# Modulation weights as eight row blocks on two DMA queues, summed block by block, at the start of a transformer-block kernel

## The chip, the cores and the metric

The kernel runs on one NeuronCore of one Trainium2 chip. The metric is the device time of one execution in microseconds (us); lower is better. A profile is one traced execution, and its span (first to last instruction) is about 1.9 us shorter than the device time of the same execution. Engine names: PE is TensorE, PEld its weight loads, DVE is VectorE, ACT is ScalarE, SP is SyncE, POOL is GpSimd. A "q" after an engine (SPq, ACTq) means its queue issuing DMA. PE and the DMA engines are the two actors of this story.

All runs below are of the fast state. They carry a second variation that matters here: the granted clock of PE over the span, between 0.992 and 1.000.

## The reference, cut to what matters

```python
mod = (silu(c) @ w_mod).reshape(1, 6, 1, -1)     # c: 1 x 1024, w_mod: 1024 x 6144, bf16
sa, ca, ga, sb, cb, gb = mod[:, 0..5]
h = layernorm(x) * (1 + ca) + sa                 # x: 2048 x 1024
x = x + ga * linear_attention(h @ wqkv) @ wo     # 32 heads
h = layernorm(x) * (1 + cb) + sb
x = x + gb * (silu(h @ w_gate) * (h @ w_up)) @ w_down
```

Nothing of the first projection can start before `sa` and `ca` are known for the rows of the contraction that it uses. Those two vectors need the first 2,048 columns of `w_mod`, 4 MB in bf16. That wait at the very start is what the change is about. (MB in the cost sums below are the loads' 1024 x 1024 bytes; KB are 1024 bytes.)

## The kernel before

The tokens are worked off in four chunks of 512; a chunk has four tiles of 128 tokens. The start-up (chunk 0) loads x tiles 0 to 2, c, and the modulation columns in *column blocks*: for each half b of the 1,024 columns and for q = 1 (ca) and q = 0 (sa), one load of all 1,024 rows by 512 columns. In such a load every contiguous piece is 1 KB.

```python
wme = [[big("wme", [DC, NB]) for _ in range(2)] for _ in range(2)]     # DC = 8, NB = 512

def load_mod(b, q, lo, hi):
    nc.sync.dma_start(out=wme[b][q][:, :, lo:hi], in_=wm_v[:, :, q * D + b * NB + lo:q * D + b * NB + hi])

load_mod(0, 1, 0, NB)      # ca, first half of the columns
load_mod(0, 0, 0, NB)      # sa, first half
load_k(0); load_k(1)       # 256 KB each: rows of wk
load_x(STC - 1, nc.sync)   # x tile 3
load_k(2); load_k(3)
load_mod(1, 1, 0, NB)      # second half of the columns, in between the rest of wk
load_mod(1, 0, 0, NB // 2)
# ... (cut)
```

PE turns silu(c) into column sums with matvecs (128x128 weights, one moving column). The column loop is outside, so a column needs all eight row groups j at once:

```python
def mod_block(b, q, lo, hi):
    for i in range(lo, hi):
        col = q * DC + 4 * b + i
        for j in range(DC):
            mm(mod_ps[:, col:col + 1], lhsT=wme[b][q][:, j, i * P:(i + 1) * P],
               rhs=scT[:, j:j + 1], start=(j == 0), stop=(j == DC - 1))
    # ... (cut: copy to ca1T with +1, or to saT)
```

With half of the columns modulated, PE starts the K projection on half of the contraction (four of eight row groups of wk, six of eight output groups), and fits the second half, and tile 3, in between:

```python
def keep_warm(acc, n):                       # warm-up matmuls: work whose result nobody reads
    for _ in range(n):
        mm(acc[:], lhsT=sel[:, 0, :], rhs=sel[:], start=True, stop=True)

# ... (cut: transposes of tiles 0 to 2, first half of the modulation)
k_mms(0, gs, accs, 0, 4)                     # 24 K matmuls
xn3 = ln1_norm(*ln1_stats(0, 3), dve=True)
pe_transpose_tile(hT, xn3, 3, DC // 2)
for cc in range(4):
    modulate(hT, cc, ca1T, saT, H, SCW)
mod_block(1, 1, 0, 4)                        # second half, between K matmuls
# ... (cut: 40 K matmuls more)
```

The start-up on VectorE, ScalarE and GpSimd is held to the program order, and in the timeline PE's matmuls stand in that order too. After the K projection of chunk 0 comes its V projection, and from there PE is never idle.

Of the kernel before, what the change touches and what calls it, by code (L numbers as in the profile page):

```python
# [8 lines left out]
ACT = mybir.ActivationFunctionType  # L9
ALU = mybir.AluOpType  # L10
BF16 = mybir.dt.bfloat16
F32 = mybir.dt.float32
# [9 lines left out]
def kernel(  # L22
# [13 lines left out]
    nc = tc.nc  # L36
    P = nc.NUM_PARTITIONS
    _, S, D = A_x.shape
# [4 lines left out]
    DC = D // P  # L43
    HG = DC
    FC = F // P
    SCW = 512
    NSC = S // SCW
    STC = SCW // P
    NB = 512
# [16 lines left out]
    wm_v = w_mod.rearrange("(j p) n -> p j n", p=P)  # L66
    c_v = c.rearrange("o (j p) -> (o j) p", p=P)

    const = ctx.enter_context(tc.tile_pool(name="const", bufs=1))
# [12 lines left out]
    @contextmanager  # L82
    def in_order(*engines):
        types = [e.engine for e in engines]
        traced = nc.cur_bb.bb.instructions
        mark = traced[-1]
        yield
        first = next(k for k in reversed(range(len(traced))) if traced[k] is mark) + 1
        for i in traced[first:]:
            if i.engine in types:  # L90
                prev = last_on.get(i.engine)
                if prev is not None:
                    tc.add_manual_dep(i, prev.name, mybir.DependencyInfo(
                        mybir.DependencyClass.NoSync, mybir.DependencyReason.DATA), reason="in_order")
                last_on[i.engine] = i

    def mm(out, lhsT, rhs, start, stop):
        return tc.keep_in_program_order(nc.tensor.matmul(out, lhsT=lhsT, rhs=rhs, start=start, stop=stop))  # L98

    def transpose(out, in_):  # L100
        return tc.keep_in_program_order(nc.tensor.transpose(out, in_, ident[:]))  # L101

    def big(name, shape):
        return k8.tile([P] + shape, BF16, name=name, tag="k8")

    def acc_a():
        return pa.tile([P, NB], F32, name="acc", tag="pa")

    def acc_b(name, shape=(NB,), dt=F32):
        return pb.tile([P] + list(shape), dt, name=name, tag="pb")  # L110
# [3 lines left out]
    c_sb = const.tile([DC, P], BF16, name="c_sb")  # L114
# [3 lines left out]
    def load_x(st, eng):  # L118
        x_sb = k2.tile([P, D], BF16, name="x_sb")
        eng.dma_start(out=x_sb[:], in_=x2[st * P:(st + 1) * P, :])  # L120
        x_tiles[st] = x_sb

    for st in range(STC - 1):
        load_x(st, nc.sync)
    nc.sync.dma_start(out=c_sb[:], in_=c_v)

    wk = [big("wk", [4, D]), big("wk", [4, D])]
    wme = [[big("wme", [DC, NB]) for _ in range(2)] for _ in range(2)]

    def load_mod(b, q, lo, hi):  # L130
        nc.sync.dma_start(out=wme[b][q][:, :, lo:hi], in_=wm_v[:, :, q * D + b * NB + lo:q * D + b * NB + hi])

    def load_k(cc):
        nc.sync.dma_start(out=wk[cc // 4][:, cc % 4, :], in_=wqkv_v[:, cc, D:2 * D])

    load_mod(0, 1, 0, NB)
    load_mod(0, 0, 0, NB)
    load_k(0)
    load_k(1)
    load_x(STC - 1, nc.sync)  # L140
    load_k(2)
    load_k(3)
    load_mod(1, 1, 0, NB)
    load_mod(1, 0, 0, NB // 2)
    load_k(4)
    load_k(5)
    load_mod(1, 0, NB // 2, NB)
    load_k(6)
    load_k(7)

    def load_w(view, lo, name):
        ts = []
# [11 lines left out]
    ident = const.tile([P, P], BF16, name="ident")  # L164
    make_identity(nc, ident[:])
    neg_half = const.tile([P, 1], F32, name="neg_half")
    nc.vector.memset(neg_half[:], -0.5)

    scT = const.tile([P, DC], BF16, name="scT")
    sc32 = const.tile([P, DC, 32], BF16, name="sc32")  # L170

    saT = const.tile([P, DC], F32, name="saT")
    ca1T = const.tile([P, DC], F32, name="ca1T")
    sbT = const.tile([P, DC], F32, name="sbT")
    cb1T = const.tile([P, DC], F32, name="cb1T")
    ga_t = ep.tile([P, NB], F32, name="e")
# [40 lines left out]
    def modulate(hT, cc, scaleT, biasT, lo=0, hi=SCW):  # L217
        nc.vector.tensor_scalar(out=hT[:, cc, lo:hi], in0=hT[:, cc, lo:hi], scalar1=scaleT[:, cc:cc + 1],  # L218
                                scalar2=biasT[:, cc:cc + 1], op0=ALU.mult, op1=ALU.add)

    def pe_transpose_tile(hT, xn, t, split):
        tp = acc_b("tp", (DC, P), BF16)
        for cc in range(DC):
            transpose(tp[:, cc, :], xn[:, cc * P:(cc + 1) * P])
        if split < DC:
            nc.scalar.copy(out=hT[:, split:DC, t * P:(t + 1) * P], in_=tp[:, split:DC, :])  # L226
        nc.vector.tensor_copy(out=hT[:, 0:split, t * P:(t + 1) * P], in_=tp[:, 0:split, :])

    hTs = {}

    def ln1_stats(sc, t):
        x_sb = x_tiles.pop(sc * STC + t)
        mv = small.tile([P, STC, 2], F32, name="mv")
        bn(x_sb, mv[:, 0, :])
        rstd = rstd_of(mv, 1)
        return sc, t, x_sb, mv, rstd

    def ln1_norm(sc, t, x_sb, mv, rstd, dve=False):
        xn = k2.tile([P, D], BF16, name="xn", bufs=4)
        if dve:  # L240
            normalise(xn[:], x_sb[:], mv[:, 0, 0:1], rstd[:, 0:1])
        else:
            normalise_act(xn[:], x_sb[:], mv, rstd)
        if sc > 0:
            nc.sync.dma_start_transpose(hTs[sc][:, :, t * P:(t + 1) * P], xn[:])
        return xn
# [3 lines left out]
        for t in range(STC):  # L250
            ln1_norm(*ln1_stats(sc, t))

    def mod_block(b, q, lo, hi):
        for i in range(lo, hi):
            col = q * DC + 4 * b + i
            for j in range(DC):
                mm(mod_ps[:, col:col + 1], lhsT=wme[b][q][:, j, i * P:(i + 1) * P],
                   rhs=scT[:, j:j + 1], start=(j == 0), stop=(j == DC - 1))
        cs = slice(4 * b + lo, 4 * b + hi)
        src = mod_ps[:, q * DC + 4 * b + lo:q * DC + 4 * b + hi]  # L260
        if q == 1:
            nc.vector.tensor_scalar_add(out=ca1T[:, cs], in0=src, scalar1=1.0)
        else:
            nc.vector.tensor_copy(out=saT[:, cs], in_=src)

    last_phi = [None]

# [11 lines left out]
    def k_mms(sc, gs, accs, cc_lo=0, cc_hi=DC):  # L279
        for cc in range(cc_lo, cc_hi):  # L280
            for (t, nb), acc in zip(gs, accs):
                mm(acc[:], lhsT=hTs[sc][:, cc, t * P:(t + 1) * P], rhs=wk[cc // 4][:, cc % 4, nb * NB:(nb + 1) * NB],
                   start=(cc == 0), stop=(cc == DC - 1))
# [129 lines left out]
    def keep_warm(acc, n):  # L413
        for _ in range(n):
            mm(acc[:], lhsT=sel[:, 0, :], rhs=sel[:], start=True, stop=True)

    gs = k_groups[0:6]
    accs = [acc_a() if i < 4 else acc_b("acc") for i in range(6)]
    spare = accs[5]
    keep_warm(spare, 11)  # L420
    hT = hTs[0] = big("hT", [DC, SCW])
    pks[0] = big("pk", [STC, D])
    H = 3 * P
    with in_order(nc.vector, nc.scalar, nc.gpsimd):
        mod_ps = acc_b("mod_ps")
        mm(mod_ps[:, 0:DC], lhsT=c_sb[:], rhs=ident[0:DC, 0:DC], start=True, stop=True)
        keep_warm(spare, 10)
        nc.scalar.activation(out=scT[:], in_=mod_ps[:, 0:DC], func=ACT.Silu)
        xns = [ln1_norm(*ln1_stats(0, t)) for t in range(3)]
        pe_transpose_tile(hT, xns[0], 0, DC)  # L430
        keep_warm(spare, 3)
        pe_transpose_tile(hT, xns[1], 1, DC)
        keep_warm(spare, 2)
        mod_block(0, 1, 0, 4)
        pe_transpose_tile(hT, xns[2], 2, DC // 2)
        keep_warm(spare, 4)
        for lo, hi in ((0, 1), (1, 4)):
            mod_block(0, 0, lo, hi)
            for cc in range(lo, hi):
                modulate(hT, cc, ca1T, saT, 0, H)  # L440
        k_mms(0, gs, accs, 0, 4)
        xn3 = ln1_norm(*ln1_stats(0, 3), dve=True)
        pe_transpose_tile(hT, xn3, 3, DC // 2)
        for cc in range(4):
            modulate(hT, cc, ca1T, saT, H, SCW)
        mod_block(1, 1, 0, 4)
        gs7, accs7 = k_groups[6:7], [acc_b("acc")]
        k_mms(0, gs7, accs7, 0, 2)
        for cc in (4, 5):
            mod_block(1, 0, cc - 4, cc - 3)  # L450
            modulate(hT, cc, ca1T, saT)
            if cc == 4:
                k_mms(0, gs7, accs7, 2, 4)
        k_mms(0, gs + gs7, accs + accs7, 4, 5)
        k_mms(0, gs[0:4], accs[0:4], 5, 6)
        mod_block(1, 0, 2, 4)
        for cc in (6, 7):
            modulate(hT, cc, ca1T, saT)
        k_mms(0, gs[4:6] + gs7, accs[4:6] + accs7, 5, 6)
        k_mms(0, gs + gs7, accs + accs7, 6, 8)  # L460
        gs8, accs8 = k_groups[7:8], [acc_b("acc")]
        k_mms(0, gs8, accs8)
        k_evac(0, gs, accs)
        k_evac(0, gs7, accs7)
        k_evac(0, gs8, accs8)
# [224 lines left out]
```

## Time and profile before

| | kernel before |
|---|---|
| device time, median of 3 runs | 839.66 us (838.86 to 839.79) |
| span of the profiled run, granted clock | 836.6 us, 1.000 |
| PE busy | 829.8 us (99%) |
| first modulation matvec | 10.33 us |
| first K matmul (reads `wk`) | 14.50 us |
| first V matmul (reads `wv`) | 31.95 us |
| from the first V matmul to the end | 804.6 us |

The head of the page of the kernel before: the span, and busy time, share and number of instructions on PE.

```profile
span 836.6 us, 11355 instructions
PE 829.8 (99%) x4701; PEld 380.7 (46%) x4701; DVE 307.6 (37%) x598; ACT 170.1 (20%) x255; POOL 60.9 (7%) x165
```

A PE that is busy for 99% of the span leaves only its start to be gained. So I read the first 60 us. The chain of waits of the kernel before in that window, in order of time (start, duration, what held the end up):

```profile
2.98 10.27 DMA wme<-in_w_mod_dram
13.30 0.37 PE mod_ps L98 x8
...
14.64 5.20 PE acc L98 x24
...
27.19 32.98 PE acc L98 x152
```

One long piece is not PE: the load of `wme` until 13.25 us. From 27.19 us on the chain is PE alone. In between, PE and its helpers alternate. The timeline of PE in the kernel before shows those alternations (start, duration, engine, line, operation, output<-inputs, shapes, count; in brackets the idle time before it and what ended that):

```profile
10.33 0.95 PE L98 MATMUL mod_ps<-scT,wme 128*128 128x1 bf16 x32 [0.20 <-DMA wme<-in_w_mod_dram]
...
13.30 0.35 PE L98 MATMUL mod_ps<-scT,wme 128*128 128x1 bf16 x8 [0.69 <-DMA wme<-in_w_mod_dram]
...
14.50 5.34 PE L98 MATMUL acc<-wk,hT 128*128 128x512 bf16 x24
19.68 0.61 PE L101 MATMUL tp<-ident,xn 128*128 128x128 bf16 x8
...
21.78 0.61 PE L98 MATMUL acc<-wk,hT 128*128 128x512 bf16 x2 [0.71 <-DVE hT L218]
...
26.34 5.76 PE L98 MATMUL acc<-wk,hT 128*128 128x512 bf16 x25
31.95 4.26 PE L98 MATMUL acc<-wv,hT 128*128 128x512 bf16 x19
```

From first K to first V 17.44 us pass.

The DMA view of the kernel before over the first 36 us, in 40 slices of 0.9 us: the busy share of the 16 DMA engines in tenths, and what they moved in GB/s.

```profile
DMA  0099978999999999999999999999999999999999
GB/s 0 11 294 298 312 248 286 329 353 316 370 383 382 391 391 379 362 355 337 315 336 361 342 329 376 382 391 394 401 389 380 391 387 405 412 410 401 407 389 412
```

The engines are busy throughout, yet between 1.8 and 9 us they move about 300 GB/s and only from 24 us, with 2 KB rows, about 390 to 410.

### The profile page before, as it was taken

How to read it: one execution, taken by the hardware profiler on the slowest of the kernel's cores; microseconds unless marked ns; L12 is line 12 of the kernel's file. 1: busy time of each engine (PE TensorE's matmuls, PEld its weight loads, DVE VectorE, ACT ScalarE, POOL GpSimd, SP SyncE). 2: the span in 40 equal slices, each digit the busy share in tenths (PEclk: the TensorE clock that was granted, in tenths of full speed). 3: DMA queues.
4: the chain of work that ended last, by engine and by line, in shares of the span. 5: the costliest groups of instructions: out<-in, count | busy, mean ns of one | idle time of the engine just before them, and what ended most of it. 6: DMA issues, size and time to landing. Idle time of an engine off the chain costs nothing.

```text
span 836.6 us, 11355 instructions
## 1 busy us (share of the span) xinstructions
PE 829.8 (99%) x4701; PEld 380.7 (46%) x4701; DVE 307.6 (37%) x598; ACT 170.1 (20%) x255; POOL 60.9 (7%) x165
## 2 busy tenths in 40 slices
PE   8999999999999999999999999999999999999998
PEld 4444444444444444444444444444444444444444
DVE  5755554587413324521111344222114431111122
ACT  3455343334211111101111110111110101111000
POOL 2011211111130001100000010000001100000000
PEclk9999999999999999999999999999999999999999
DMA  9894890029997446337434173672505529710011
GB/s 311 305 253 100 254 213 2 13 68 239 366 243 262 151 151 207 120 99 229 150 102 151 45 221 100 201 239 62 189 1 127 188 69 322 241 60 0 13 64 51
DMA packets 127668, 129.34 MB, mean 155 GB/s; under 512 B 33920, under 2 KB 109184, under 8 KB 127104
## 3 DMA queue, kind: packets, MB, share of 16 engines
q1 hardware_dynamic: 123568, 115.36, 45.7%
q0 software_dynamic: 4048, 13.25, 5.4%
q8 instruction: 37, 0.61, 0.3%
q14 instruction: 15, 0.12, 0.1%
HBM read 108.53 MB, written 12.72 MB: 145 GB/s over the span
## 4 chain that ended last, share of the span: by engine, by line
PE 97%; DMA 1%; DVE 1%; SPq 0%; ACT 0%; issue 0%
PE acc L98 89%; PE a_ps L98 7%; DMA wme<-in_w_mod_dram 1%; PE kvp L98 1%; PE modr L98 0%; PE den L98 0%; PE mod_ps L98 0%; DVE hT L218 0%; SPq L120 0%; DVE wo L528 0%; PE wf L98 0%; DVE pq L273 0%; ACT eb L270 0%; ACT hT L226 0%; PE tp L101 0%
## 5 line engine op out<-in xcount | busy, mean ns | idle before, releaser
L98 PE MATMUL acc<-h2T,wgu 128*128 128x512 bf16 x1792 | 387.6, 379 | 0.0
L98 PEld LDWEIGHTS <-wgu 128*128 128x128 bf16 x1792 | 175.3, 98 | 211.3
L98 PE MATMUL acc<-wd,gu 128*128 128x512 bf16 (+2 forms) x924 | 196.1, 373 | 0.0
L597 DVE TENSOR_TENSOR gu<-acc,e 128x512 bf16<-128x512 f32 x112 | 77.5, 692 | 299.2 <-PE acc L98 296.5
L596 ACT ACTIVATE e<-acc 128x512 f32<-128x512 f32 x112 | 66.9, 597 | 374.8 <-PE acc L98 374.8
L98 PEld LDWEIGHTS <-gu 128*128 128x128 bf16 x924 | 89.3, 98 | 104.4
L98 PEld LDWEIGHTS <-hT 128*128 128x128 bf16 x512 | 49.2, 98 | 60.4 <-DVE hT L218 1.5
L618 DVE TENSOR_TENSOR e<-acc,gb_bc 128x512 f32<-128x512 f32 (+2 forms) x33 | 22.3, 675 | 131.9 <-PE acc L98 131.9
L98 PE MATMUL acc<-wk,hT 128*128 128x512 bf16 x256 | 57.6, 379 | 0.8 <-DVE hT L218 0.7
L98 PE MATMUL a_ps<-wo,pq 128*128 128x512 bf16 x256 | 57.4, 379 | 0.0
L98 PE MATMUL acc<-hT,wq 128*128 128x512 bf16 x256 | 56.8, 379 | 0.0
L98 PE MATMUL acc<-wv,hT 128*128 128x512 bf16 x256 | 55.9, 379 | 0.0
L270 ACT ACTIVATE eb<-acc 128x512 bf16<-128x512 f32 x64 | 37.9, 595 | 66.2 <-PE acc L98 63.1
L215 ACT ACTIVATE xn<-x,nmr,rstd 128x1024 bf16<-128x1024 f32 x16 | 19.8, 1240 | 126.3 <-POOL nmr L213 126.3
L565 POOL DMA_DIRECT2D x_scratch<-x x16 | 9.7, 608 | 418.5 <-DVE x L558 418.5
L98 PEld LDWEIGHTS <-pq 128*128 128x128 bf16 x256 | 25.0, 98 | 30.2
L98 PEld LDWEIGHTS <-wq 128*128 128x128 bf16 x256 | 24.6, 98 | 29.8 <-issue 0.9
L271 DVE TENSOR_SCALAR eb<-eb 128x512 bf16<-128x512 bf16 x64 | 18.4, 292 | 49.0 <-ACT eb L270 49.0
L558 DVE TENSOR_TENSOR x<-a_ps,x_sb 128x512 f32<-128x512 f32 x32 | 22.1, 691 | 7.9 <-PE a_ps L98 7.8
L199 POOL TENSOR_TENSOR rstd<-veps,neg_half 128x1 f32<-128x1 f32 x32 | 17.9, 559 | 75.3 <-DVE veps L197 72.9
L308 ACT CAST v<-acc 128x512 bf16<-128x512 f32 x32 | 18.3, 582 | 23.1 <-PE acc L98 23.0
L621 DVE TENSOR_TENSOR ob<-e,x1r 128x512 bf16<-128x512 f32 (+2 forms) x33 | 22.3, 675 | 1.0
(70 smaller groups left out, 263.1 us busy)
## 6 DMA issues: line engine op xcount, KB each, us to landing
wgu<-in_B_w_gate_dram SPq DMA_DIRECT2D x28, 1024.0 KB, 7.9
wgu<-in_B_w_up_dram SPq DMA_DIRECT2D x28, 1024.0 KB, 8.7
x_sb<-in_A_x_dram SPq DMA_DIRECT2D x32, 256.0 KB, 6.8
wml<-in_w_mod_dram SPq DMA_DIRECT2D x8, 1024.0 KB, 8.7
x_scratch<-x POOLq DMA_DIRECT2D x16, 512.0 KB, 3.0
x1r<-x_scratch SPq DMA_DIRECT2D x31, 256.0 KB, 2.8
wd<-in_B_w_down_dram SPq DMA_DIRECT2D x7, 1024.0 KB, 6.0
rbc<-rden_scratch POOLq DMA_DIRECT2D x16, 256.0 KB, 5.4
```

The lines of the kernel that those rows point to most:

```text
L98: return tc.keep_in_program_order(nc.tensor.matmul(out, lhsT=lhsT, rhs=rhs, start=start, stop=stop))
L199: nc.gpsimd.tensor_tensor(out=rstd[:, 0:n], in0=veps[:, 0:n], in1=neg_half[:].to_broadcast([P, n]), op=ALU.pow)
L215: nc.scalar.activation(out=dst, in_=src, func=ACT.Identity, bias=nmr[:], scale=rstd[:, 0:1])
L270: nc.scalar.activation(out=e[:], in_=acc, func=ACT.Exp)
L271: nc.vector.tensor_scalar(out=e[:], in0=e[:], scalar1=1.0, scalar2=PHI_EPS, op0=ALU.min, op1=ALU.add)
L308: nc.scalar.copy(out=v[:, t * D + nb * NB:t * D + (nb + 1) * NB], in_=acc[:])
L558: nc.vector.tensor_tensor(out=x1[:, ns], in0=a_ps[:], in1=x_t[:, ns], op=ALU.add)
L565: nc.gpsimd.dma_start(out=x1_dram[st * P:(st + 1) * P, :], in_=x1[:])
L596: nc.scalar.activation(out=sg[:], in_=ps[0][:], func=ACT.Silu)
L597: gm = nc.vector.tensor_tensor(out=guT[sc][f // GPT][:, f % GPT, :], in0=ps[1][:], in1=sg[:], op=ALU.mult)
L618: nc.vector.tensor_tensor(out=yt, in0=y_ps, in1=gb_bc[:, ns], op=ALU.mult)
L621: nc.vector.tensor_tensor(out=ob, in0=yt, in1=x1r, op=ALU.add)
```

## The change

Intent: longer rows (4 KB instead of 1 KB) for the loads that everything waits for, two issuing queues, and matvecs that are summed as each block of rows lands, so that little is left to do when the last block is there. All modulation now comes before the first K matmul; K then runs without interruption but for the transposes of tile 3, whose modulation reads PSUM directly. The diff, cut to its core:

```diff
-    for st in range(STC - 1):
-        load_x(st, nc.sync)
-    nc.sync.dma_start(out=c_sb[:], in_=c_v)
+    load_x(0, nc.sync)
+    load_x(1, nc.scalar)
+    load_x(2, nc.sync)
+    nc.scalar.dma_start(out=c_sb[:], in_=c_v)
-    wme = [[big("wme", [DC, NB]) for _ in range(2)] for _ in range(2)]
+    wme = [big("wme", [2, 2 * D]) for _ in range(DC // 2)]
# ... (cut: the old interleaved loads)
+    for j in range(DC):
+        (nc.sync, nc.scalar)[(j + 1) % 2].dma_start(out=wme[j // 2][:, j % 2, :], in_=wm_v[:, j, 0:2 * D])
+    for cc in range(4):
+        load_k(cc)
     load_x(STC - 1, nc.sync)
+    for cc in range(4, DC):
+        load_k(cc)
# ...
+    def mod_block(j):
+        for col in range(2 * DC):
+            mm(mod_ps[:, col:col + 1], lhsT=wme[j // 2][:, j % 2, col * P:(col + 1) * P], rhs=scT[:, j:j + 1],
+               start=False, stop=(j == DC - 1 and col == 2 * DC - 1))
# ... the start-up
+        mm(mod_ps[:, 0:2 * DC], lhsT=ident[:], rhs=base[:], start=True, stop=False)
# ... (cut: silu, normalisation, the helper turn)
+        keep_warm(spare, 5)
+        mod_block(0)
+        keep_warm(spare, 2)
+        mod_block(1)
+        turn(0)                       # transposes of tile 0 and their copy
+        keep_warm(spare, 1)
+        mod_block(2)
+        keep_warm(spare, 1)
+        turn(1)
+        keep_warm(spare, 2)
+        mod_block(3)
+        keep_warm(spare, 2)
+        turn(2)
+        mod_block(4)
+        for j in range(5, DC):
+            keep_warm(spare, 4)
+            mod_block(j)
+        nc.vector.tensor_copy(out=sca[:], in_=mod_ps[:, 0:2 * DC])
+        for cc in range(DC):
+            modulate(hT, cc, ca1T, saT, 0, H)
+        k_mms(0, gs, accs, 0, 6)
+        xn3 = ln1_norm(*ln1_stats(0, 3), dve=True)
+        tp3 = pe_transpose_tile(xn3)
# ... (cut: tile 3 modulated from tp3; the rest of K)
```

More of the change, by code (lines that the diff above doesn't have):

```diff
@@ L121, in load_x @@
         x_tiles[st] = x_sb
-    for st in range(STC - 1):
-        load_x(st, nc.sync)
-    nc.sync.dma_start(out=c_sb[:], in_=c_v)
+    load_x(0, nc.sync)
+    load_x(1, nc.scalar)
+    load_x(2, nc.sync)
+    nc.scalar.dma_start(out=c_sb[:], in_=c_v)
     wk = [big("wk", [4, D]), big("wk", [4, D])]
-    wme = [[big("wme", [DC, NB]) for _ in range(2)] for _ in range(2)]
-    def load_mod(b, q, lo, hi):
-        nc.sync.dma_start(out=wme[b][q][:, :, lo:hi], in_=wm_v[:, :, q * D + b * NB + lo:q * D + b * NB + hi])
+    wme = [big("wme", [2, 2 * D]) for _ in range(DC // 2)]
     def load_k(cc):
         nc.sync.dma_start(out=wk[cc // 4][:, cc % 4, :], in_=wqkv_v[:, cc, D:2 * D])
-    load_mod(0, 1, 0, NB)
-    load_mod(0, 0, 0, NB)
-    load_k(0)
-    load_k(1)
+    for j in range(DC):
+        (nc.sync, nc.scalar)[(j + 1) % 2].dma_start(out=wme[j // 2][:, j % 2, :], in_=wm_v[:, j, 0:2 * D])
+    for cc in range(4):
+        load_k(cc)
     load_x(STC - 1, nc.sync)
-    load_k(2)
-    load_k(3)
-    load_mod(1, 1, 0, NB)
-    load_mod(1, 0, 0, NB // 2)
-    load_k(4)
-    load_k(5)
-    load_mod(1, 0, NB // 2, NB)
-    load_k(6)
-    load_k(7)
+    for cc in range(4, DC):
+        load_k(cc)
     def load_w(view, lo, name):
@@ L167 @@
     nc.vector.memset(neg_half[:], -0.5)
+    base = const.tile([P, 2 * DC], BF16, name="base")
+    nc.vector.memset(base[:, 0:DC], 0.0)
+    nc.vector.memset(base[:, DC:], 1.0)
     scT = const.tile([P, DC], BF16, name="scT")
     sc32 = const.tile([P, DC, 32], BF16, name="sc32")
-    saT = const.tile([P, DC], F32, name="saT")
-    ca1T = const.tile([P, DC], F32, name="ca1T")
+    sca = const.tile([P, 2 * DC], F32, name="sca")
+    saT, ca1T = sca[:, 0:DC], sca[:, DC:2 * DC]
     sbT = const.tile([P, DC], F32, name="sbT")
@@ L219, in modulate, with pe_transpose_tile @@
                                 scalar2=biasT[:, cc:cc + 1], op0=ALU.mult, op1=ALU.add)
-    def pe_transpose_tile(hT, xn, t, split):
+    def pe_transpose_tile(xn):
         tp = acc_b("tp", (DC, P), BF16)
@@ L224, in pe_transpose_tile @@
             transpose(tp[:, cc, :], xn[:, cc * P:(cc + 1) * P])
-        if split < DC:
-            nc.scalar.copy(out=hT[:, split:DC, t * P:(t + 1) * P], in_=tp[:, split:DC, :])
-        nc.vector.tensor_copy(out=hT[:, 0:split, t * P:(t + 1) * P], in_=tp[:, 0:split, :])
+        return tp
     hTs = {}
@@ L251, in ln1 @@
             ln1_norm(*ln1_stats(sc, t))
-    def mod_block(b, q, lo, hi):
-        for i in range(lo, hi):
-            col = q * DC + 4 * b + i
-            for j in range(DC):
-                mm(mod_ps[:, col:col + 1], lhsT=wme[b][q][:, j, i * P:(i + 1) * P],
-                   rhs=scT[:, j:j + 1], start=(j == 0), stop=(j == DC - 1))
-        cs = slice(4 * b + lo, 4 * b + hi)
-        src = mod_ps[:, q * DC + 4 * b + lo:q * DC + 4 * b + hi]
-        if q == 1:
-            nc.vector.tensor_scalar_add(out=ca1T[:, cs], in0=src, scalar1=1.0)
-        else:
-            nc.vector.tensor_copy(out=saT[:, cs], in_=src)
+    def mod_block(j):
+        for col in range(2 * DC):
+            mm(mod_ps[:, col:col + 1], lhsT=wme[j // 2][:, j % 2, col * P:(col + 1) * P], rhs=scT[:, j:j + 1],
+               start=False, stop=(j == DC - 1 and col == 2 * DC - 1))
     last_phi = [None]
@@ L425 @@
         mod_ps = acc_b("mod_ps")
-        mm(mod_ps[:, 0:DC], lhsT=c_sb[:], rhs=ident[0:DC, 0:DC], start=True, stop=True)
-        keep_warm(spare, 10)
-        nc.scalar.activation(out=scT[:], in_=mod_ps[:, 0:DC], func=ACT.Silu)
+        mm(mod_ps[:, 2 * DC:3 * DC], lhsT=c_sb[:], rhs=ident[0:DC, 0:DC], start=True, stop=True)
+        mm(mod_ps[:, 0:2 * DC], lhsT=ident[:], rhs=base[:], start=True, stop=False)
+        nc.scalar.activation(out=scT[:], in_=mod_ps[:, 2 * DC:3 * DC], func=ACT.Silu)
@@ L429 @@
         xns = [ln1_norm(*ln1_stats(0, t)) for t in range(3)]
-        pe_transpose_tile(hT, xns[0], 0, DC)
-        keep_warm(spare, 3)
-        pe_transpose_tile(hT, xns[1], 1, DC)
-        keep_warm(spare, 2)
-        mod_block(0, 1, 0, 4)
-        pe_transpose_tile(hT, xns[2], 2, DC // 2)
-        keep_warm(spare, 4)
-        for lo, hi in ((0, 1), (1, 4)):
-            mod_block(0, 0, lo, hi)
-            for cc in range(lo, hi):
-                modulate(hT, cc, ca1T, saT, 0, H)
-        k_mms(0, gs, accs, 0, 4)
@@ L442 @@
-        xn3 = ln1_norm(*ln1_stats(0, 3), dve=True)
-        pe_transpose_tile(hT, xn3, 3, DC // 2)
-        for cc in range(4):
-            modulate(hT, cc, ca1T, saT, H, SCW)
-        mod_block(1, 1, 0, 4)
-        gs7, accs7 = k_groups[6:7], [acc_b("acc")]
-        k_mms(0, gs7, accs7, 0, 2)
-        for cc in (4, 5):
-            mod_block(1, 0, cc - 4, cc - 3)
-            modulate(hT, cc, ca1T, saT)
-            if cc == 4:
-                k_mms(0, gs7, accs7, 2, 4)
-        k_mms(0, gs + gs7, accs + accs7, 4, 5)
@@ L455, with turn @@
-        k_mms(0, gs[0:4], accs[0:4], 5, 6)
-        mod_block(1, 0, 2, 4)
-        for cc in (6, 7):
-            modulate(hT, cc, ca1T, saT)
-        k_mms(0, gs[4:6] + gs7, accs[4:6] + accs7, 5, 6)
-        k_mms(0, gs + gs7, accs + accs7, 6, 8)
+        def turn(t):
+            tp = pe_transpose_tile(xns[t])
+            nc.vector.tensor_copy(out=hT[:, :, t * P:(t + 1) * P], in_=tp[:])
+        keep_warm(spare, 5)
+        mod_block(0)
+        keep_warm(spare, 2)
+        mod_block(1)
+        turn(0)
@@ L461 @@
+        tp3 = pe_transpose_tile(xn3)
+        for cc in range(DC):
+            nc.vector.tensor_scalar(out=hT[:, cc, H:SCW], in0=tp3[:, cc, :], scalar1=ca1T[:, cc:cc + 1],
+                                    scalar2=saT[:, cc:cc + 1], op0=ALU.mult, op1=ALU.add)
+        k_mms(0, gs, accs, 6, DC)
+        gs7, accs7 = k_groups[6:7], [acc_b("acc")]
+        k_mms(0, gs7, accs7)
         gs8, accs8 = k_groups[7:8], [acc_b("acc")]
```

## The prediction

> **What bounds the kernel now.** The page gives PE 829.8 us busy of 836.6 us (99%), and the timeline no PE gap after 27.2 us: a dense matmul stream behind a start-up. The change can only move the start of that stream. I mark it by the first V matmul (wv) at 31.95 us; what follows should shift as a block.
>
> In the start-up the chain of waits has one large piece that is not PE: DMA of wme, 2.98 to 13.25 us. The first K matmul (wk) starts at 14.50 us, on two of the modulation loads (2 MB). The 64 K matmuls alone take 64 x 0.218 = 14.0 us, yet 17.4 us pass from first K to first V: 3.4 us are chunk-3 transposes with their copies and modulates, 64 mod matvecs (1.8 us) and waits.
>
> **What the change removes, adds, moves.**
> - It removes most of these interruptions: all modulation precedes the first K matmul; only 8 transposes (0.61 us) stay between. Chunk-3 modulates read PSUM and hide behind 12 K matmuls (2.6 us). K to V becomes 14.6 to 14.9 us: a gain of about 2.7 us.
> - It puts bytes ahead of the first K matmul: 0.75 MB of x and 4 MB of modulation, where 2.75 MB were enough. At the rate of the 2 KB-row weight loads in the DMA view (380 to 407 GB/s between 24 and 32 us), 2 MB take 5.3 us.
> - It gains on DMA. Now the first mod load's 16 engine landings spread from 7.69 to 10.52 us, as several engines sit without packets around 4.4 to 6.7 us when the 1 KB-row loads begin; the first 10 us move 250 to 350 GB/s. Rows of 4 KB need a quarter of the packets, so I expect 390 GB/s after the x tiles and a skew under 1 us. The second queue adds no bandwidth: the Trainium skill, "DMA: Bandwidth & Descriptors", section "Issuing engines are not separate DMA queues", runs all queues on the same 16 engines. ScalarE pays 6 x 0.43 us (SyncE's issue time) before its table load; its silu waits until 5.59 us anyway.
>
> Estimate: x landed by 4.9 us, as now; 4.19 MB at 0.39 MB/us gives 15.7; with skew block 7 lands near 16 us. Then 4 warm-up matmuls queued ahead (partly exposed, up to 0.9 us), 16 matvecs (0.5 us), a copy and a modulate (0.65 us): first K near 17.6 us, V near 32.4 us, +0.4 us. Later weights are no limit: a wk slice arrives in 0.7 us and feeds 6 matmuls, 1.3 us.
>
> **Predicted: 840.1 us, range 837.8 to 842.5. Faster by over 2%: 0.01; within 2%: 0.98; slower by over 2%: 0.01.** Two per cent is 17 us, more than the start-up can give.
>
> **What would show each step.**
> - DMA: 4 KB packets; last wme landing at 15 to 17 us; 380 to 400 GB/s from 5 us.
> - Timeline: first wk matmul 16.5 to 19 us, then K without gaps but the transposes; K to V 14.6 to 15 us.
> - Everything after the first V matmul lasts as before within 0.5 us.
> - Granted clock 1.00; K matmuls every 0.22 us.
>
> **What would make it wrong.**
> - PE cools while it waits for blocks ("TensorE: Matmul & The Clock Gate", Part 1, has an idle window of about 3.4 us halving the clock): up to +2 us.
> - Engines lag by 2 us or more with 4 KB rows too: +2 us.
> - Landings are even and early (14.5 us): -1.5 us.
> - The queues hinder each other, or ScalarE is held at issue and normalises late: +1 to 2 us.

## The result, and the profile after

The changed kernel took 841.86 us (median of 4 runs, 840.63 to 842.62) beside 839.26 us for the kernel before (4 runs). The ratio is 1.0031, 95% interval 1.0014 to 1.0049. (A ratio is the mean time of one kernel's runs over that of the other's in the same rounds, so not quite the ratio of the medians.) A later session with five rounds gave 841.66 against 838.90 us, ratio 1.0038. So the change costs 2.6 to 2.8 us, about 0.3%: inside the predicted range, "same" at the 2% mark, and yet a loss clear of noise, where the prediction's sum had come to 0.4 us.

The head of the page after:

```profile
span 840.1 us, 11368 instructions
PE 832.0 (99%) x4708; PEld 382.1 (45%) x4708; DVE 307.4 (37%) x597; ACT 168.7 (20%) x253; POOL 60.6 (7%) x165
```

The stream behind the start-up is unchanged: first V matmul to the end takes 805.0 us (804.6 before). The loss is in the first 35 us. The chain of waits of the changed kernel in the first 60 us:

```profile
2.20 9.26 DMA wme<-in_w_mod_dram
...
11.51 0.56 PE mod_ps L98 x16
12.07 0.45 PE acc L98
12.52 0.85 PE tp L101 x8
...
16.30 0.89 PE acc L98 x4
...
20.41 0.39 DVE hT L212
20.85 7.94 PE acc L98 x36
```

Here is the surprise. The load leaves the chain at 11.46 us, when block 2, the third that PE takes, has landed. Of the 9.4 us from there to the first K matmul the chain is PE's own list but for the last 0.75 us, and pieces named `acc` before 20.85 us are warm-up matmuls. The timeline of PE in the changed kernel tells why the list was so late and so long:

```profile
8.96 0.55 PE L98 MATMUL mod_ps<-scT,wme 128*128 128x1 bf16 x16 [1.97 <-DMA wme<-in_w_mod_dram]
...
12.31 1.06 PE L101 MATMUL tp<-ident,xn 128*128 128x128 bf16 x8
13.16 1.06 PE L98 MATMUL acc<-sel 128*128 128x512 bf16 x2
...
18.69 1.02 PE L98 MATMUL acc<-sel 128*128 128x512 bf16 x4
19.55 0.54 PE L98 MATMUL mod_ps<-scT,wme 128*128 128x1 bf16 x16
20.85 7.94 PE L98 MATMUL acc<-wk,hT 128*128 128x512 bf16 x36 [0.76 <-DVE hT L212]
28.63 0.61 PE L101 MATMUL tp<-ident,xn 128*128 128x128 bf16 x8
29.08 6.21 PE L98 MATMUL acc<-wk,hT 128*128 128x512 bf16 x28
35.12 1.24 PE L98 MATMUL acc<-wv,hT 128*128 128x512 bf16 x5
```

PE waited 1.97 us for block 0. The eight transposes at 12.31 us took 1.06 us instead of the 0.61 us at 19.68 us of the kernel before, since the clock had dropped. The windows view of the changed kernel (busy time and instructions of each engine in a stretch, then the granted clock, DMA share and GB/s):

```profile
12.00:15.20 3.20, 3.20 (x32) 1.92 (x30) 0.69 (x1) 0.05 (x1) 0.00 (x0) 0.50 1.02 402
```

The clock was 0.50 between 12.00 and 15.20 us; the trace's clock records put the whole stretch at 11.90 to 15.31 us.

The load itself did what the prediction asked of it. GB/s in the same 0.9 us slices as above, now of the changed kernel:

```profile
GB/s 0 9 189 364 421 412 369 419 410 414 419 423 423 405 414 407 380 387 376 391 266 259 346 241 191 264 344 364 405 428 382 380 389 391 380 391 394 376 394 357
```

Between 3.6 and 14.4 us it moved 405 to 423 GB/s in all slices but one. But look at the order in which the blocks came. The trace has one landing for each of the 16 DMA engines of a load; I took for every block the 13th and the last of them (us):

```
block (queue)      13th     last       PE starts its matvecs
0 (ScalarE)        8.36     8.91        8.96
1 (SyncE)          6.73     7.28        9.80
2 (ScalarE)       10.94    11.46       11.51
3 (SyncE)          9.32     9.83       14.02
4 (ScalarE)          -     14.02       15.76
5 (SyncE)         11.88    12.39       17.02
6 (ScalarE)       15.68    17.65       18.28
7 (SyncE)         14.49    14.95       19.55
```

(Block 4 shares its semaphore with c, so I give only its last landing.) Every odd block, on SyncE, landed before the even one that PE had to take first. And of the last block to land, block 6, 15 engines were done by 15.97 us and one at 17.65 us. PE came to block 6 at 18.28 us, so although the load is not on the chain of this run, it was only 0.6 us from being so.

The sum of the start-up, by the two marks:

| | before | predicted | after | after, second profile |
|---|---|---|---|---|
| first K matmul | 14.50 | 17.6 | 20.85 | 20.08 |
| K to V | 17.44 | 14.6 to 14.9 | 14.27 | 14.27 |
| first V matmul | 31.95 | 32.4 | 35.12 | 34.35 |
| half-speed stretch before V | none | none | 11.90 to 15.31 | none |

K to V gained 3.17 us; the first K matmul lost 6.35 us (5.58 us where the clock held).

### The profile page after: what moved, and what is told of

Read it like the earlier page. It is cut to its first block, busy times and chain, and to the rows that moved or that the text cites. A ratio compares the mean times of both kernels' runs of the same rounds, so it can differ in the third digit from the quotient of the medians.

```text
span 840.1 us, 11368 instructions
## 1 busy us (share of the span) xinstructions
PE 832.0 (99%) x4708; PEld 382.1 (45%) x4708; DVE 307.4 (37%) x597; ACT 168.7 (20%) x253; POOL 60.6 (7%) x165
## 3 DMA queue, kind: packets, MB, share of 16 engines
q0 software_dynamic: 4048, 13.25, 5.3%
## 4 chain that ended last, share of the span: by engine, by line
PE 98%; DMA 1%; DVE 0%; ACTq 0%; ACT 0%; issue 0%; DVEq 0%
PE acc L98 89%; PE a_ps L98 7%; DMA wme<-in_w_mod_dram 1%; PE kvp L98 1%; PE modr L98 0%; PE mod_ps L98 0%; PE den L98 0%; PE tp L101 0%; DVE wo L515 0%; PE wf L98 0%; DVE pq L257 0%; ACT eb L254 0%; ACTq L126 0%; ACTq L135 0%; DVE hT L212 0%
## 5 line engine op out<-in xcount | busy, mean ns | idle before, releaser
L193 POOL TENSOR_TENSOR rstd<-veps,neg_half 128x1 f32<-128x1 f32 x32 | 17.9, 559 | 77.6 <-DVE veps L191 75.3
```

The lines of the kernel that those rows point to most:

```text
L193: nc.gpsimd.tensor_tensor(out=rstd[:, 0:n], in0=veps[:, 0:n], in1=neg_half[:].to_broadcast([P, n]), op=ALU.pow)
```

## The experiments

Twelve experiments ran (nine kernels and three repeats), in three sessions with five rounds each; each session had 11 runs of the kernel before (medians 838.37, 838.87 and 838.90 us). All gave correct results. Theory: after the third block PE's own fixed list sets the first K matmul (warm-up matmuls, the order of the blocks, the lost clock), and bandwidth does not. Rivals: the late landing of the blocks sets it; two queues are slower than one; the row length is of no account.

### 1. Without the late warm-up matmuls

```diff
         for j in range(5, DC):
-            keep_warm(spare, 4)
             mod_block(j)
```

> The changed kernel without the 12 warm-up matmuls before blocks 5, 6 and 7. Theory 1 (after about 11.5 us PE works through its own fixed list, and the filler in that list is what delays the first K matmul): 12 x 0.222 us = 2.7 us less work, so the first K matmul moves from 20.85 us to the landing of the last block plus about 1.2 us, 17 to 19.2 us, and the time falls by 1.6 to 2.7 us. Rival (the late landing of the blocks sets it, the filler only fills waits): the first K matmul stays within 0.5 us of 20.85 us and the time within 0.5 us. If the clock drops without the filler, the first K matmuls come at 0.43 us and up to 1.7 us are given back.

The timeline of PE in this run, then the windows view:

```profile
15.18 1.90 PE L98 MATMUL mod_ps<-scT,wme 128*128 128x1 bf16 x64
17.83 9.63 PE L98 MATMUL acc<-wk,hT 128*128 128x512 bf16 x36 [0.76 <-DVE hT L212]
...
33.79 2.54 PE L98 MATMUL acc<-wv,hT 128*128 128x512 bf16 x11
```

```profile
18.00:21.40 3.40, 3.40 (x9) 1.22 (x8) 3.23 (x10) 0.00 (x0) 0.00 (x0) 0.51 1.05 386
```

The first K matmul came 3.0 us earlier, at 17.83 us (20.85 us before the edit). The edit alone doesn't explain all of it: the 12 matmuls are worth 2.7 us, block 0 landed 0.5 us earlier in this run, and the last block landed at 16.07 us instead of 17.65 us, which the edit doesn't touch. From that landing to the first K matmul 1.76 us passed; with the last block at 17.65 us the first K matmul would have been near 19.4 us (an estimate). So the list did delay it, but without the list the load is the next limit, close behind. And 36 K matmuls now took 9.63 us instead of 7.94 us, as the clock fell to half between 18.05 and 21.46 us. K to V grew to 15.96 us. (A first half-speed stretch, 11.22 to 14.63 us, came here as well, after a wait of 1.78 us for block 0.) Over five runs the clock share was 0.992 to 0.996 and the time 842.43 us, ratio 1.0051; the profiled run was the fastest of them. The filler both costs and guards; taking it out moves the cost, it does not remove it.

### 2. One queue

```diff
-    load_x(1, nc.scalar)
+    load_x(1, nc.sync)
-    nc.scalar.dma_start(out=c_sb[:], in_=c_v)
+    nc.sync.dma_start(out=c_sb[:], in_=c_v)
-        (nc.sync, nc.scalar)[(j + 1) % 2].dma_start(...)
+        nc.sync.dma_start(...)
```

> The changed kernel with every early load on the SyncE queue, in the order x0, x1, x2, c, blocks 0 to 7. If the second queue matters for the rate, the eight blocks land at less than 400 GB/s and the last one later than 15.7 us (its 13th engine in the changed kernel); if only the 4 KB rows matter, the rate stays at 400 to 420 GB/s. If the order of landing matters (with two queues block 1 landed at 7.28 us before block 0 at 8.91 us, and block 3 before block 2), the first block now lands by about 7.3 us, PE waits less than 1 us before it, the clock does not drop to 0.5, and the time falls by 1 to 1.5 us against the changed kernel.

The timeline of PE in this run:

```profile
7.59 0.54 PE L98 MATMUL mod_ps<-scT,wme 128*128 128x1 bf16 x16
...
17.27 0.55 PE L98 MATMUL mod_ps<-scT,wme 128*128 128x1 bf16 x16 [0.41 <-DMA wme<-in_w_mod_dram]
18.58 7.94 PE L98 MATMUL acc<-wk,hT 128*128 128x512 bf16 x36 [0.76 <-DVE hT L212]
...
32.85 3.40 PE L98 MATMUL acc<-wv,hT 128*128 128x512 bf16 x15
```

Blocks landed in order, the first at 7.32 us, then one each 1.28 to 1.41 us up to block 6 at 15.21 us (512 KB in 1.28 us is 410 GB/s, the same rate as with two queues). Block 7 had 15 engines done by 16.50 us and the last at 17.22 us: an engine trailed with one queue as well. PE met block 0 without a wait, no stretch at half speed came, and the first K matmul was at 18.58 us, 2.3 us earlier than in the changed kernel. Here the load is the last to end again: PE waited 0.41 us for block 7. Time 839.66 us, ratio 1.0015 (1.0003 to 1.0027).

### 3. Queues swapped

```diff
-        (nc.sync, nc.scalar)[(j + 1) % 2].dma_start(...)
+        (nc.sync, nc.scalar)[j % 2].dma_start(...)
```

> The changed kernel with even blocks on SyncE and odd blocks on ScalarE, so that the blocks land in the order in which PE takes them. Theory (PE stood still from 6.99 to 8.96 us for block 0 while block 1 had been there since 7.28 us, and the clock window that followed went to 0.5): first matvecs at 7.3 to 7.5 us, no window at 0.5, first K matmul 1 to 2 us earlier, time 1 to 2 us less. Rival (order is of no account because the filler list sets the end): same first K matmul within 0.5 us.

First matvecs at 7.62 us, no half-speed stretch before V, last landing at 16.68 us, first K matmul at 18.41 us, first V at 32.68 us. The profiled run agrees with the theory. The six timed runs scatter more, 839.19 to 843.20 us with clock shares of 0.996 to 1.000; median 840.06 us, ratio 1.0026 (1.0010 to 1.0041).

### 4. More warm-up before block 0

```diff
-        keep_warm(spare, 5)
+        keep_warm(spare, 14)
         mod_block(0)
```

> The changed kernel with 14 instead of 5 warm-up matmuls before block 0, nothing else: PE stays busy from 5.7 to 8.9 us. Theory (the half-speed window at 11.90 to 15.31 us comes of the 2 us wait before block 0, and costs about 1.4 us): granted clock 1.0 after 5 us, transposes of chunk 1 in 0.61 us instead of 1.06 us, first K matmul about 19.4 us, time 1.2 to 1.5 us less. Rival (the window comes of the later small gaps): a window at 0.5 stays, no gain.

The timeline of PE in this run:

```profile
9.41 0.54 PE L98 MATMUL mod_ps<-scT,wme 128*128 128x1 bf16 x16
...
19.17 7.94 PE L98 MATMUL acc<-wk,hT 128*128 128x512 bf16 x36 [0.76 <-DVE hT L212]
```

No half-speed stretch in the profile, the transposes of tile 1 again 0.61 us, first K matmul at 19.17 us. (The last block landed at 16.30 us here, 1.35 us earlier than in the changed kernel's profile, and PE did not wait for it; so part of the 1.7 us is chance.) Four of five runs had a clock share of 0.999 or more (changed kernel: two of nine). Time 840.66 us, ratio 1.0029 (1.0017 to 1.0041). That fits the theory that the wait before block 0 brings the stretch; not every such wait does, as experiment 10 had one of 1.48 us and no stretch. The time is 1.2 us below the changed kernel's first measurement, but that was another session, and 14 matmuls end after block 0 landed, so a part is given back: the first matvec is at 9.41 us.

### 5. One queue and no late warm-up

The edits of 1 and 2 together.

> The one-queue variant without the 12 warm-up matmuls before blocks 5, 6 and 7. In the one-queue variant PE waited 0.41 us for the last block (17.22 us), so there the load sets the first K matmul. Theory (with the list short enough, landing is the limit and filler only guards the clock): first K matmul unchanged within 0.5 us of 18.58 us unless the last block itself lands earlier, but a half-speed window appears within the first K matmuls, K to V grows from 14.27 to about 16 us, and the time is 1 to 2 us worse than with the filler. Rival (filler costs wherever it stands): first K matmul 1 us or more earlier and the time better by 1 us.

The first K matmul was at 18.25 us (18.58 us with the filler), so there the filler cost next to nothing. But half speed came at 15.21 us and lasted two stretches, 6.83 us; K to V was 16.13 us, and the time 841.70 us, ratio 1.0037. The theory holds, the rival falls.

### 6. One queue, 1 KB rows

```diff
-    for j in range(DC):
-        nc.sync.dma_start(out=wme[j // 2][:, j % 2, :], in_=wm_v[:, j, 0:2 * D])
+    for i in range(DC // 2):
+        for lo in range(0, 2 * D, NB):
+            nc.sync.dma_start(out=wme[i][:, :, lo:lo + NB], in_=wm_v[:, 2 * i:2 * i + 2, lo:lo + NB])
```

> The one-queue variant with the same blocks fetched in pieces of 1 KB rows (16 loads of 256 KB, each 2 blocks by 512 columns); order on PE the same. Theory (row length sets the rate: 512 KB took 1.28 us with 4 KB rows, about 410 GB/s; the kernel before moved 1 MB of 1 KB rows in 2.99 us, about 350 GB/s): the last block lands 1.7 to 2.2 us later than 17.2 us, the first K matmul at 20.3 to 20.8 us, time 2 us worse than the one-queue variant. Rival (the old loads were slow for their place and size, not for their rows): the same landing within 0.5 us.

Successive loads of 256 KB landed 0.75 us apart (350 GB/s, against 410 with 4 KB rows), and the last of them at 19.33 us, 2.1 us later than the last block of experiment 2. The edit halves the size of a load too, but that isn't what counts: the kernel before had 350 GB/s with 1 MB loads of 1 KB rows, and the 256 KB loads of `wk`, with 2 KB rows, have 390. So row length does set the rate. The first K matmul was at 21.66 us, later than expected, as waits in the first blocks brought two half-speed stretches (9.35 to 16.17 us); 842.99 us, ratio 1.0048. The size of the time loss therefore mixes both, and only the rate is clean.

### 7. The kernel before, on two queues

```diff
+    load_x(1, nc.scalar)   # was nc.sync; c too
-    load_mod(0, 0, 0, NB)
+    load_mod(0, 0, 0, NB, nc.scalar)
```

> The kernel before, with x1, c and one of the two first modulation loads issued by ScalarE instead of SyncE, nothing else. Theory (the second queue carries no bandwidth of its own): the two first loads share the engines, the later of them lands within 0.7 us of 13.25 us, the earlier one lands later than 10.28 us, and the time is the same within 1 us or worse by up to 1 us since the first matvecs start later. Rival (the spread of 2.8 us between engines in the first load came of one queue feeding descriptors slowly): the later load lands before 12.2 us, the first K matmul moves from 14.5 to about 13.3 us, the time falls by up to 1 us.

Worse: 842.30 us, ratio 1.0039. The two first modulation loads landed at 10.71 and 14.37 us (10.28 and 13.25 us before), while wk slices 0 and 1, issued after them on SyncE, landed at 11.81 and 12.57 us, earlier than before (13.94 and 14.59 us). With its queue one load shorter, SyncE reached the wk loads while ScalarE's load was still under way, and they took bandwidth from the load that PE waited for. The first K matmul was at 15.62 us, and a half-speed stretch at 24.09 us stretched K to V to 18.81 us. The rival (one queue fed the engines too slowly) falls. My own expectation missed too: the later load came 1.1 us after 13.25 us, not within 0.7, and the time rose by 3.4 us, not by 1 us at most.

### 8 and 9. Half-column row blocks, a try at something better

Both keep one queue and block-by-block sums, but take half of the columns first, as the kernel before does, so that K can start after 2 MB. Core of the edit:

```diff
+    for i in range(4):
+        load_mod(0, i)      # two loads of 2 row groups x 512 columns, 1 KB rows
+    load_k(0); load_k(1); load_mod(1, 0); load_k(2); load_x(STC - 1, nc.sync)
+    load_mod(1, 1); load_k(3); load_mod(1, 2); load_mod(1, 3)
```

> A try at a better kernel: row blocks and accumulation block by block as in the change, but for half of the columns first (as in the kernel before), one queue, in loads of 256 KB with 1 KB rows; the second half of the modulation is loaded between the wk slices. Expected if the loads flow at about 350 GB/s: first half landed near 11 us, first K matmul near 12.3 us (14.5 before), a wait of up to 2 us for the second half near 20 us, first V matmul near 29.5 us (31.95 before), time 1.5 to 2.5 us below the kernel before. If the engines spread by 2 us again or the clock drops in the waits: no gain.

(The profile is of the slowest of the six runs, 843.86 us.) First K matmul at 13.47 us, but K ran dry: PE stood 1.98 us for wk slice 3, which landed at 19.46 us behind modulation loads. Three half-speed stretches followed, and the first V matmul came at 36.46 us. 841.21 us, ratio 1.0026. My load order was wrong. The second form loads wk slices 0 to 3 and x tile 3 ahead of the second half:

> The half-block kernel with the first four wk slices and the fourth x tile loaded ahead of the second half of the modulation (in its first form PE stood 2 us waiting for the fourth wk slice, which landed at 19.46 us behind modulation loads, and three half-speed windows followed). Expected: no wait before the first 24 K matmuls end at about 18.8 us, second half landed near 22.5 us as before, first V matmul at 31 to 32 us against 31.95 us in the kernel before: time within 1 us of the kernel before. If the clock drops in the wait for the second half: 1 to 2 us worse.

The timeline of PE in the second form:

```profile
13.39 5.35 PE L98 MATMUL acc<-wk,hT 128*128 128x512 bf16 x23 [0.90 <-DVE hT L223]
...
22.36 0.45 PE L98 MATMUL mod_ps<-scT,wme 128*128 128x1 bf16 x12 [0.49 <-DMA wme<-in_w_mod_dram]
23.52 7.94 PE L98 MATMUL acc<-wk,hT 128*128 128x512 bf16 x35 [0.71 <-DVE hT L223]
31.31 4.91 PE L98 MATMUL acc<-wv,hT 128*128 128x512 bf16 x22
```

V at 31.31 us is 0.64 us better than the kernel before, and this profiled span is 836.3 us. Over five runs, though, the clock share was 0.995 to 1.000 and the time 840.69 us, ratio 1.0019 (1.0006 to 1.0031). Device time minus span was 2.1 to 3.3 us here, and as much in experiment 8, against 1.7 to 2.2 us in the kernel before; why, I can't say. No version of mine beat the kernel before.

### 10 to 12. The changed kernel, one queue and swapped queues side by side

The three kernels unaltered, on one chip.

> The changed kernel, unaltered, to stand beside the next two runs on the same chip. Expected: 2 to 3.5 us over the kernel before, as in the first measurement; in the profile again a wait of about 2 us before block 0 and a window at half speed after it.

> The one-queue variant again. If the order in which two queues deliver is what costs beyond the price of the bytes, it is 1 to 2 us faster than the changed kernel of the same call and its runs have a granted clock of 1.0 more often; the first K matmul again near 18.6 us. Rival (the difference between the two was chance of chip and day): both within 0.5 us.

> The variant with the two queues swapped again. If order alone is it, this is as fast as the one-queue variant within 0.7 us and 1 to 2 us faster than the changed kernel of the same call; first K matmul near 18.4 us. Rival: no faster than the changed kernel.

The medians were 841.66, 840.14 and 841.14 us, the ratios 1.0038, 1.0021 and 1.0028. The changed kernel's second profile had no half-speed stretch, against my expectation, and so shows what is left without one. Its timeline of PE:

```profile
8.74 0.55 PE L98 MATMUL mod_ps<-scT,wme 128*128 128x1 bf16 x16 [1.48 <-DMA wme<-in_w_mod_dram]
...
17.50 0.55 PE L98 MATMUL mod_ps<-scT,wme 128*128 128x1 bf16 x16 [0.74 <-DMA wme<-in_w_mod_dram]
17.92 1.02 PE L98 MATMUL acc<-sel 128*128 128x512 bf16 x4
18.78 0.54 PE L98 MATMUL mod_ps<-scT,wme 128*128 128x1 bf16 x16
20.08 7.94 PE L98 MATMUL acc<-wk,hT 128*128 128x512 bf16 x35 [0.76 <-DVE hT L212]
```

In this run PE did wait for block 6 (landed at 17.46 us), with block 7 there since 15.04 us; after block 6 it still had four warm-up matmuls and block 7 to do, and the first K matmul came 2.6 us after the landing. In experiment 2, where block 7 landed last, it came 1.4 us after. So the order of the blocks costs at the end as well. And in this run the load stays on the chain until 17.46 us: that PE's own list set the end in the first profile was one of two cases, not the rule.

One queue repeated its first profile: first K matmul at 18.15 us (18.58 us before), no half-speed stretch in the start-up. The swapped queues did not repeat theirs. In the second one late DMA engines delivered block 0 at 9.02 us (13th engine: 6.75 us):

```profile
9.07 0.55 PE L98 MATMUL mod_ps<-scT,wme 128*128 128x1 bf16 x16 [2.57 <-DMA wme<-in_w_mod_dram]
...
21.93 7.94 PE L98 MATMUL acc<-wk,hT 128*128 128x512 bf16 x35 [0.76 <-DVE hT L212]
```

A wait of 2.57 us, then two half-speed stretches (10.91 to 17.73 us), and the first K matmul at 21.93 us. So the order of the queues alone does not keep block 0 from coming late. That the swap is faster than the changed kernel is not shown (0.5 us between medians of runs that scatter by 3 us). That one queue is faster is supported, not proven: 1.5 us between the medians of the shared session and 1.3 us between the means, with ratios whose 95% intervals overlap (1.0024 to 1.0052, 1.0006 to 1.0035); the spans below, which pool sessions and chips, differ by 1.55 us.

Mean spans of all timed runs, by clock (each line pools two sessions, the kernel before three; the changed kernel's first session is that of the result, which is not one of the three):

```
                     runs  mean span   runs with clock >= 0.999   their mean span
kernel before         33     836.76              19                  836.37
changed kernel         9     839.92               2                  839.05
one queue             11     838.37               8                  837.76
queues swapped        12     839.09               7                  837.96
```

The changed kernel loses 3.2 us of span to the kernel before. At the full clock it loses 2.7 us (only two runs), one queue 1.4 us. So of the 3.2 us about half goes with the second queue (order of landing, and the clock that falls in the waits). The rest I put down to the price of the bytes: with one queue, where the load sets the pace, all 4 MB still come before the first K matmul and the saved interruptions don't quite pay for that. This second half is argued from the timelines; no run changes the bytes alone.

## Why the prediction was right or wrong

- **Total, 840.1 us with 837.8 to 842.5: held** (841.86 us), on the slow side. The reasoning that 2% is out of reach held too. But the sum behind it gave a loss of 0.4 us, and 2.6 us were measured; the total lies in the range because the range left room for the risks that were listed, not because the sum was right.
- **The stream after the first V matmul is unchanged: right**, 805.0 against 804.6 us.
- **DMA with 4 KB rows at about 390 GB/s: right, and a little low.** 405 to 423 GB/s. Experiment 6 confirms that row length is the cause: 350 against 410 GB/s in the same place. (The landings of 7.69 to 10.52 us in the prediction are counted from an origin 0.24 us earlier; from the start of the span they are 7.45 to 10.28 us.) Experiment 2 confirms what the Trainium skill says in "DMA: Bandwidth & Descriptors", "Issuing engines are not separate DMA queues": one queue reaches the same 410 GB/s.
- **K to V 14.6 to 14.9 us: mechanism right, size off by 0.3 to 0.6 us.** It was 14.27 us in every run of this K order whose clock held during K: 64 matmuls of 0.216 us and 0.45 us on the chain for the eight transposes, where the prediction had 0.218 and 0.61 us.
- **"With skew block 7 lands near 16 us", skew under 1 us: the first step that failed.** In the changed kernel 15 engines of the last block were done by 15.97 us, as predicted, but one landed at 17.65 us; in the second profile the 13th landed at 15.98 us and the last at 17.46 us. PE needs all 16. Over the profiles that kept two queues and 4 KB rows the last landing lay between 16.07 and 17.65 us, so this term was too small by up to 1.6 us.
- **"Then 4 warm-up matmuls queued ahead (partly exposed, up to 0.9 us), 16 matvecs": the second step that failed.** I took block 7 to land last, and PE to be waiting for it with everything else done. But block 6 landed last in both profiles, and after it PE's list still had block 6, four warm-up matmuls and block 7. In the second profile the first K matmul came 2.6 us after that landing, where the prediction has 1.6 us from 16 to 17.6 us. In the first profile PE was behind its blocks as well: it began block 5 4.6 us after its landing and block 7 4.6 us after. Had PE been waiting, the first K matmul of that run would have come at about 20.3 us (an estimate: the last landing 17.65 us and the 2.6 us of the second profile); it came at 20.85 us, so being behind cost only about 0.6 us more. Two things had put PE behind. Blocks landed in another order than PE takes them, since SyncE's loads ran ahead of ScalarE's; I had treated the landing as one moment. And the wait of 1.97 us for block 0 was followed by a half-speed stretch. The prediction named the cooling as a risk worth up to 2 us; in the chain of waits it is about 1.5 us (transposes 0.85 instead of 0.45 us, warm-up matmuls 0.43 instead of 0.22 us each), most of which the late landing of block 6 would have cost anyway. In the second profile, without it, PE did wait for block 6, and the exposed work was two blocks of matvecs and all four warm-up matmuls, 1.7 us instead of the 0.5 to 1.4 us of the prediction.
- **First K matmul 17.6 us: wrong**, 20.85 and 20.08 us, by the sum of those two steps: in the first profile 1.65 us of landing, 1.0 us of work behind it and 0.6 us of being behind. Experiments 1, 2 and 4 moved it by 3.0, 2.3 and 1.7 us from the first profile, but their last landings were earlier too (16.07, 17.22 and 16.30 us), and two profiles of one kernel can lie 0.8 us (changed kernel) or 3.5 us (queues swapped) apart. Of the variants only one queue has a second profile that agrees. So these experiments show which terms there are; how much each is worth in a typical run stays open.
- **"ScalarE is held at issue": true, but harmless as far as I can see.** Its six DMA issues kept it until 5.38 us, the table load began at 5.40 us and the silu at 6.70 us (5.59 us before), still ahead of the first block.

The timeline of ScalarE in the changed kernel for that last point:

```profile
1.73 3.65 ACTq L135 DMA_DIRECT2D wme<-in_w_mod_dram  x4
5.40 1.28 ACT L412 ACT_TABLE_LOAD   x1 [5.40 <-DMA x_sb<-in_A_x_dram]
6.70 0.18 ACT L412 ACTIVATE scT<-mod_ps 128x8 bf16<-128x8 f32 x1
```

Left open: why one DMA engine falls behind. In the changed kernel a 16 KB packet of the instruction queue ran from 15.41 us for 1.04 us, and in block 6 and the six loads after it one engine's landing came about 1.4 us or more after the other 15. Every run here has such a packet, between 13.3 and 17.9 us, and in at least five others (experiments 6, 7, 9, 10 and 11) the last landing falls back just after it. No run here takes that packet away, so it is a guess at the cause, not a finding.

## What to carry to other kernels

When an engine takes its work in a fixed order, spreading its inputs over two queues can change the order in which they land; unless the program's order follows, the engine waits for one block while the next lies ready. Filler that keeps the matmul clock up is part of the critical path as soon as the engine is behind, and removing it can cost as much as it saves, so first remove the wait that made it necessary. And a faster load is worth only what it brings forward: here 4 KB rows raised the rate from 350 to 410 GB/s, but all 4 MB instead of 2 MB had to come first, which by the sums above took that back. Last, one profile of a start-up is one case: compare the landings of two runs before putting a difference down to the edit.

## What the Trainium skill lacked or had wrong

- "DMA: Bandwidth & Descriptors", specifications table: it asks for at least 512 B for line rate. On one queue, 256 KB loads in 1 KB rows landed 0.75 us apart (350 GB/s), 256 KB wk loads in 2 KB rows about 0.67 us apart (390 GB/s), and 512 KB loads in 4 KB rows 1.28 us apart (410 GB/s): well above 512 B the row length still counts for 17%.
- The same page, "Issuing engines are not separate DMA queues": right on bandwidth (410 GB/s on one queue as on two) and in that the loads interleave, but the section does not say that dividing loads over two queues changes which load lands first, which cost time here. Block 1 landed at 7.28 us and block 0 at 8.91 us; in experiment 7 two later wk loads overtook the modulation load that PE waited for (11.81 and 12.57 us against 14.37 us).
- "TensorE: Matmul & The Clock Gate", Part 1: it has the clock fall after at least one idle window of about 3.4 us. The half-speed stretches here are 3.41 us long or a multiple, as the page says of its window, but they came without any idle stretch of that length: the waits before one were 1.97 us in the changed kernel (half speed from 11.90 us) and 2.57 us with the queues swapped (from 10.91 us), and in experiment 5 half speed began at 15.21 us in a stretch of matvecs with waits of 0.52 and 0.72 us. Part 1 also has the clock oscillate when PE idles briefly but frequently between groups of matmuls, which is nearer to what is seen here; it gives no length for those idles, and how much one-column matvecs count as activity is on no part of the page that I found.
- No page that I found has by how much one DMA engine can trail the other 15 of the same load: 1.7 us between the 15th and the last landing of block 6 in the changed kernel (15.97 and 17.65 us). "DMA: Bandwidth & Descriptors" lists two engines, 7 and 15, as usually slower than the others; the landings in these traces don't name their engine, so whether it is one of them is not shown.
